# Splitting matmuls into column halves: gate and value products of one token block, down products of the next

## Chip, cores and metric

The kernel runs on one core of a Trainium2 chip. The metric is the device time of one execution in microseconds (us), as a median of several runs. A separate profiled execution gives the rows that are shown below.

## What is computed

Attention over four sequences of 768 tokens with eight heads of 64, and a gated MLP on its output. Each query sees the keys less than 16 positions away, and one pooled key (maximum) and value (mean) per block of 32 positions. The MLP takes the 3072 tokens of 512 features to 1536 and back. Cut to what matters:

```python
x = attention(q, k, v)                      # 3072 tokens x 512
g = x @ w_gate                              # 3072 x 1536
silu = g * (1.0 / (1.0 + np.exp(-g)))
val = x @ w_val
out = (silu * val) @ w_out                  # 3072 x 512
```

## The kernel before

The 3072 tokens go in six blocks k = 0 to 5 of TOK = 512. Within a block, attention leaves x transposed: features on the 128 partitions, in NP = 4 tiles u, the 512 tokens along the free dimension. Each tile is held as a rounded part `xh` and the rest `xl`, both fp32r (a 4-byte type that TensorE takes in a single pass). The weights are held in the same two parts, `wh` and `wl`, and a product is made of three terms: `wl·xh`, `wh·xl`, `wh·xh`.

The 1536 hidden features go in NJ = 12 tiles j of 128. For each (k, j):

- `m_gate` calls `m_up` (L609) for the gate product: 4 tiles u with 3 terms each, 12 matmuls (L619) that add up in one PSUM tile `g` of 128 x 512. The weights are the stationary operand (128 x 128), x the moving one (512 token columns). ScalarE then applies Silu to the whole tile (L625) and leaves `a` in SBUF.
- `m_val` does the same with the value weights into a tile `v`, multiplies `a` by it on VectorE (L630), rounds `a` to `ah` on ScalarE (through the helper at L187) and leaves the rest `al` on GpSimd (helper at L183).
- `m_down` (L660) multiplies `ah` and `al` with the 128 rows of w_out that belong to j: for each of NTP = 4 groups i of 128 tokens three terms, 12 matmuls (L669). Here the activations are stationary and w_out is the moving operand with DM = 512 output columns. The sums stay in four PSUM tiles `acc` over all twelve j; after j = 11 they are copied out and stored.

From block 1 on a loop writes the order by hand: gate (k, j), some attention steps of a later block, value (k, j), more attention steps, the down products of the (k, j) before, and again attention steps. A manual dependency on every instruction keeps this order on each engine. Block 0 follows a list of steps of its own. The attention steps for block k + 1 lie between the products of block k; block 5 has none.

PSUM has two buffers for g and v (`psg`), two for attention (`psy`) and four for the sums (`psc`). The weights stay in SBUF for the whole run; those of j = 11 lie in a pool of their own (`wts3`), opened late, and the gate and value weights of j = 0 and 11 are separate tiles (`w_g`, `w_v`) where the other j share one (`w_gv`).

Every matmul in the program comes with a weight load (LDWEIGHTS, engine PEld in the profile). At the start, and while the first attention steps wait, the kernel runs fillers: matmuls of a tile of plain fp32 zeros with 128 to 512 columns (`zeros`, L693).

Of the kernel before, what the change touches and what calls it, by code (L numbers as in the profile page):

```python
# [18 lines left out]
DM = H * D  # L19
DFF = 1536  # L20
BLK, WIN = 32, 16
P = 128
NP = H // 2
# [9 lines left out]
TOK = 512  # L33
# [3 lines left out]
NJ = DFF // P  # L37
# [3 lines left out]
WARM = (4, 3)  # L41
OWN = (0,)
SHORT = 2
QC = P // NP
ODD = NT // 2
EVEN = 1 + ODD
# [33 lines left out]
def blocks_of(k):  # L80

    return [(b, pos, i * QT // SQ + x, n * QT // SQ) for x, (b, pos, i, n) in enumerate(parts_of(k))]


def parts_of(k):


    found, at = [], k * TOK
    while at < (k + 1) * TOK:
        b, pos = divmod(at, S)  # L90
        n = min(S - pos, (k + 1) * TOK - at)
        found.append((b, pos, (at - k * TOK) // QT, n // QT))
        at += n
    return found


def value_pool() -> np.ndarray:

    m = np.zeros((P, NV, QC), np.float32)
    for i in range(WIN, WIN + S):  # L100
# [62 lines left out]
def body(ctx, tc, qP, kP, vT, vP, kq, kF, qF, vE, vR, vO, wgv, wends, wo, cst_in, bias_in, out):  # L163
    nc = tc.nc
# [20 lines left out]
    def copy(e, out, in_):  # L185
        if e == "a":
            nc.scalar.copy(out, in_)  # L187
        else:
            (nc.vector if e == "d" else nc.gpsimd).tensor_copy(out, in_)
# [64 lines left out]
    KT, VT, ksum, vsum, X, U = {}, {}, {}, {}, {}, {}  # L254
# [39 lines left out]
    def a_load_windows(k, u):  # L294
        if k >= SHORT:
            parts = blocks_of(k)
            kw = two.tile([P, TOK // SQ + len(parts), SB], F32, tag="kw", name=f"kw_{k}_{u}")
            for b, pos, i, n in parts:
                nc.sync.dma_start(
                    kw[:, i : i + n + 1, :SQ],  # L300
                    kP[b, u][:, pos : pos + (n + 1) * SQ].rearrange("p (n j) -> p n j", j=SQ),
                )
            U.setdefault((k, u), {})["kw"] = kw
            return
        kw = two.tile([P, NT, KC], F32, tag="kw", name=f"kw_{k}_{u}")
        for b, pos, i, n in parts_of(k):
            src = kP[b, u]
            nc.sync.dma_start(
                kw[:, i : i + n, :KW], bass.AP(src.tensor, src.offset + pos, [[PADS, P], [QT, n], [1, KW]])
            )  # L310
        U.setdefault((k, u), {})["kw"] = kw
# [29 lines left out]
    def a_keys(k, u):  # L341
        for b, pos, i, n in parts_of(k) if k < SHORT else blocks_of(k):
            if pos == 0:
                a_pool_keys(u, 0)
            kw = U[k, u]["kw"]
            copy(
                "p",
                kw[:, i : i + n, KW:] if k < SHORT else kw[:, i : i + n, SQ:],
                ksum[u].rearrange("p (o n) -> p o n", o=1).broadcast_to([P, n, NB]),
            )  # L350
# [23 lines left out]
    def v_rows():  # L374
        if "rows" not in vn:
            t = pro.tile([P, (EVEN + NV - 1) * DM + NV * QC], F32, name="vrows")
            vn["flat"] = t
            vn["rows"] = t[:, : (EVEN + NV - 1) * DM].rearrange("p (n d) -> p n d", d=DM)
        return vn["rows"]

    def v_even(i):
        return 0 if i == NV - 1 else EVEN + i

    def v_sums():
# [3 lines left out]
        for i in range(NV):  # L388
            n = P if i < NV - 1 else VREST
            for u in range(NP):  # L390
                nc.tensor.matmul(  # L391
                    ps[u * QC : (u + 1) * QC, :P], mean_sb[:n, i, :], v_rows()[:n, v_even(i), u * P : (u + 1) * P],
                    start=i == 0, stop=i == NV - 1,
                )

    def v_keep():

        ps = vn.pop("sums")
        for u in range(NP):
            copy(on, vsum["all"][KW:, u * P : (u + 1) * P], ps[u * QC : u * QC + NB, :P])  # L400

# [9 lines left out]
    def a_scores(k, u):  # L411
        t = U[k, u]
        sc = [a_bank(k, u, f"sc{h}", "yg"[h]) for h in range(2)]
        t["sc"] = sc
        if k >= SHORT:
            for b, pos, at, n in blocks_of(k):
# [48 lines left out]
    def a_max(k, u, g):  # L465

        t = U[k, u]
        if g == 0 and k >= SHORT:
            t["p"] = short["p"]
# [6 lines left out]
        for c in range(NTP):  # L476
            i = g * NTP + c
            n = (k * NTP + c) % (S // P)
            kc = KC if k < SHORT else SC
            v = 0 if n == 0 else 2 if n == S // P - 1 else 1  # L480
# [126 lines left out]
    A, ACC = {}, {}  # L607

    def m_up(k, j, nm, pairs=range(NP)):  # L609

        if pairs[0] == 0:
            A[nm, k, j] = psg.tile([P, 512], F32, tag="b", name=f"{nm}_{k}_{j}")
        ps = A[nm, k, j]
        wh, wl = W[nm, j]
        for u in pairs:
            xh, xl = X[k, u]
            cs = slice(u * P, (u + 1) * P)
            for n, (w, x) in enumerate(((wl, xh), (wh, xl), (wh, xh))):
                nc.tensor.matmul(  # L619
                    ps, w[:, cs], x, start=u == 0 and n == 0, stop=u == NP - 1 and n == 2  # L620
                )
# [22 lines left out]
    def m_up_gate(k, j, *u):  # L644
        m_up(k, j, "g", *([u] if u else []))

    def m_up_val(k, j, *u):
        m_up(k, j, "v", *([u] if u else []))
# [11 lines left out]
    def m_down(k, j):  # L660
        if j == 0:
            ACC[k] = [psc.tile([P, DM], F32, tag="b", name=f"acc{i}_{k}") for i in range(NTP)]
        ah, al = A.pop((k, j))
        wh, wl = W["o", j]
        for i in range(NTP):
            ts = slice(i * P, (i + 1) * P)
            terms = ((al, wh), (ah, wl), (ah, wh)) if k < NBLK - 1 else ((ah, wh), (ah, wl), (al, wh))
            for n, (a, w) in enumerate(terms):
                nc.tensor.matmul(  # L669
                    ACC[k][i], a[:, ts], w, start=j == 0 and n == 0, stop=j == NJ - 1 and n == 2  # L670
                )
            if j == NJ - 1:
                r = k * TOK + i * P
                parts = 2 if k == NBLK - 1 and i == NTP - 1 else 1
                for h in range(parts):
                    n = DM // parts
                    cs = slice(h * n, (h + 1) * n)
                    if parts == 1:
                        o = mlp.tile([P, n], F32, tag="o", bufs=3, name=f"o_{k}_{i}")
                    else:  # L680
                        o = mlp.tile([P, TOK], F32, tag="a", name=f"o_{k}_{i}_{h}")[:, :n]
                    copy("ad"[(i + h) % 2], o, ACC[k][i][:, cs])
                    nc.sync.dma_start(out[r : r + P, cs], o)
# [76 lines left out]
    for n in WARM:  # L760
# [10 lines left out]
        "out": a_out, "outp": a_out_pooled, "split": a_split, "rest": a_rest, "w_load": w_load, "w_abs": w_abs, "w_c1": w_range,  # L771
        "w_c2": w_shift, "w_s1": w_top, "w_s2": w_rest, "w_hi": w_hi, "w_lo": w_lo, "gate": m_up_gate,
        "silu": m_silu, "val": m_up_val, "mul": m_mul, "ah": m_high, "al": m_low, "down": m_down,
        "values": a_values, "load_values": a_load_values, "keys": a_keys, "pool_values": a_pool_values,
        "exp": a_exp, "norm": a_norm,
# [48 lines left out]
    for n, (k, j) in enumerate(seq):  # L824
        m_gate(k, j)
        do(3 * n)
        m_val(k, j)
        do(3 * n + 1)
        if prev:
            m_down(*prev)  # L830
        do(3 * n + 2)
        prev = (k, j)
    m_down(*prev)
    assert not at
    for x in traced[n_before:]:
# [48 lines left out]
```

## Time and profile before

| | |
|---|---|
| median of 3 runs | 678.6 us (678.54 to 678.86) |
| time of the profiled execution | 678.02 us |
| span of the profiled execution, first to last instruction | 676.2 us |
| mean granted TensorE clock | 0.999 of full speed |
| PE (TensorE matmul) busy | 670.1 us |
| PEld (weight load) busy | 543.5 us |
| DVE (VectorE) busy | 331.3 us |
| ACT (ScalarE) busy | 298.1 us |
| POOL (GpSimd) busy | 134.4 us |

The span leaves out what lies around the program, 1.8 us here. Matmuls overlap in the record, because the recorded duration of one holds its latency; how densely they stand is read from their starts.

### The profile page before, as it was taken

The page shows a single profiled execution, that of the slowest core. Times are in us where ns is not written, and L with a number is a line of the kernel's source. Part 1 is how long each engine was busy: PE and PEld are TensorE (multiplying, and loading weights), DVE is VectorE, ACT ScalarE, POOL GpSimd, SP SyncE. Part 2 cuts the span into 40 slices and gives each one's busy share as a digit, 9 for nine tenths or more (in the row PEclk, how much of TensorE's full clock was granted, in tenths as well). Part 3 has the DMA queues.
Part 4 walks back from the last instruction along what each step waited for, and adds up shares of the span by engine and source line. Part 5 has one row for each costly group of instructions (what it writes and reads, how often), then busy time and mean ns, then how long its engine had stood idle before and what let it go on. Part 6 is the DMA issues. An engine that isn't in the chain of part 4 may idle for free.

```text
span 676.2 us, 12388 instructions
## 1 busy us (share of the span) xinstructions
PE 670.1 (99%) x4940; PEld 543.5 (80%) x4940; DVE 331.3 (49%) x919; ACT 298.1 (44%) x729; POOL 134.4 (20%) x130
## 2 busy tenths in 40 slices
PE   8999999999999999999999999999999999999997
PEld 5688888888888888888888888888888888888886
DVE  6999999946624525435346345343352451100011
ACT  6968998844441433424415424235244151211112
POOL 3110112112221212212112122121212121111110
PEclk9999999999999999999999999999999999999999
DMA  8899165145320223302404312012122000100001
GB/s 328 340 373 354 49 234 171 46 120 157 79 58 0 56 48 95 82 24 55 105 24 143 80 49 58 18 38 64 56 57 57 0 25 0 63 1 0 1 0 63
DMA packets 72058, 60.36 MB, mean 89 GB/s; under 512 B 42144, under 2 KB 60064, under 8 KB 70464
## 3 DMA queue, kind: packets, MB, share of 16 engines
q1 hardware_dynamic: 72000, 59.57, 28.6%
q8 instruction: 39, 0.64, 0.4%
q14 instruction: 19, 0.16, 0.1%
HBM read 53.26 MB, written 6.29 MB: 88 GB/s over the span
## 4 chain that ended last, share of the span: by engine, by line
PE 97%; DVE 2%; DMA 1%; issue 0%; SPq 0%; ACT 0%; DVEq 0%; ACTq 0%
PE g L619 30%; PE acc L669 29%; PE v L619 29%; PE xo L584 4%; PE sc L423 2%; DMA kq<-in_kF 1%; PE pp L537 1%; DVE p L481 1%; PE sc L434 1%; PE xo L592 1%; DVE ks L336 0%; PE pv L391 0%; PE pp L693 0%; PE pv L370 0%; DVE m_g L221 0%
## 5 line engine op out<-in xcount | busy, mean ns | idle before, releaser
L669 PE MATMUL acc<-w_o,ah 128*128 128x512 f32 x576 | 177.7, 390 | 0.0
L619 PE MATMUL g<-xh,w_gv 128*128 128x512 f32 x480 | 160.3, 395 | 0.0
L619 PE MATMUL v<-xh,w_gv 128*128 128x512 f32 x480 | 158.0, 390 | 0.0
L183 POOL TENSOR_TENSOR al<-a,ah 128x512 fp32r<-128x512 f32 x63 | 81.7, 1296 | 333.4 <-ACT ah L187 333.4
L630 DVE TENSOR_TENSOR a<-v,a 128x512 f32<-128x512 f32 x72 | 49.7, 690 | 191.6 <-PE v L619 190.8
L669 PEld LDWEIGHTS acc<-w_o,ah 128*128 128x128 f32 x576 | 108.1, 188 | 22.7
L187 ACT CAST ah<-a 128x512 fp32r<-128x512 f32 x71 | 44.0, 621 | 156.8 <-DVE a L630 156.8
L669 PE MATMUL acc<-w_o,al 128*128 128x512 f32 x288 | 113.0, 392 | 0.0
L619 PEld LDWEIGHTS g<-xh,w_gv 128*128 128x128 f32 x480 | 90.1, 188 | 21.1 <-ACT w_o L187 0.2
L619 PEld LDWEIGHTS v<-xh,w_gv 128*128 128x128 f32 x480 | 90.1, 188 | 19.1 <-issue 0.3
L625 ACT ACTIVATE a<-g 128x512 f32<-128x512 f32 x72 | 43.0, 597 | 137.9 <-PE g L619 136.3
L565 DVE STREAM_TRANSPOSE pt_short<-p_short 32x256 f32<-32x256 f32 x192 | 83.8, 436 | 25.9 <-POOL p_short L522 23.2
L619 PE MATMUL g<-xl,w_gv 128*128 128x512 f32 x240 | 93.5, 390 | 0.0
L619 PE MATMUL v<-xl,w_gv 128*128 128x512 f32 x240 | 93.4, 389 | 0.0
L669 PEld LDWEIGHTS acc<-w_o,al 128*128 128x128 f32 x288 | 54.1, 188 | 11.5 <-issue 0.2
L619 PEld LDWEIGHTS v<-xl,w_gv 128*128 128x128 f32 x240 | 45.1, 188 | 9.3
L619 PEld LDWEIGHTS g<-xl,w_gv 128*128 128x128 f32 x240 | 45.1, 188 | 8.8
L496 ACT ACTIVATE p_short<-p_short,nm 128x88 f32<-128x88 f32 x128 | 45.3, 355 | 0.2
L522 POOL TENSOR_TENSOR p_short<-p_short,ri 128x704 f32<-128x704 f32 x16 | 21.8, 1364 | 57.5 <-DVE ri L514 53.6
L619 PE MATMUL g<-xh,w_g 128*128 128x512 f32 x96 | 32.6, 400 | 0.0
L619 PE MATMUL v<-xh,w_v 128*128 128x512 f32 x96 | 31.9, 393 | 0.0
L187 ACT CAST xh<-xo 128x512 fp32r<-128x512 f32 x23 | 13.4, 591 | 38.2 <-PE xo L584 38.2
(108 smaller groups left out, 690.9 us busy)
## 6 DMA issues: line engine op xcount, KB each, us to landing
raw_gv<-in_wgv SPq DMA_DIRECT2D x10, 1024.0 KB, 11.8
raw_o<-in_wo SPq DMA_DIRECT2D x12, 512.0 KB, 7.4
out<-o SPq DMA_DIRECT2D x23, 256.0 KB, 2.0
kt<-in_kP SPq DMA_DIRECT2D x12, 384.0 KB, 4.1
vt<-in_vT SPq DMA_DIRECT2D x12, 384.0 KB, 3.9
vw<-in_vP SPq DMA_DIRECT2D x12, 384.0 KB, 3.8
kw<-in_kP SPq DMA_DIRECT2D x12, 272.0 KB, 4.7
vw<-in_vP SPq DMA_DIRECT2D x16, 192.0 KB, 3.4
```

Source lines behind the costliest of these rows:

```text
L183: (nc.vector if e == "d" else nc.gpsimd).tensor_tensor(out=out, in0=a, in1=b.bitcast(F32), op=ALU.subtract)
L187: nc.scalar.copy(out, in_)
L423: nc.tensor.matmul(sc[h][s * SQ : (s + 1) * SQ, c * SC : (c + 1) * SC], t["q"][hs, i * SQ : (i + 1) * SQ], keys[hs], start=True, stop=True,)
L434: nc.tensor.matmul(sc[h][s * QT : (s + 1) * QT, c * KC : (c + 1) * KC], t["q"][hs, qs], t["kw"][hs, i, :], start=True, stop=True,)
L496: nc.scalar.activation(out=t["p"][:, i, :kc], in_=t["p"][:, i, :kc], func=AF.Exp, scale=-1.0, bias=t["nm"][:, i : i + 1], accum_out=t["sm" ...
L522: (nc.vector if on == "d" else nc.gpsimd).tensor_tensor(out=p, in0=p, in1=ri.rearrange("p (n o) -> p n o", o=1).broadcast_to([P, 2 * NTP, ...
L565: nc.vector.transpose(out=to[r * SQ : (r + 1) * SQ, :, s * SQ : (s + 1) * SQ], in_=t["p"][s * SQ : (s + 1) * SQ, :, at : at + SQ],)
L584: nc.tensor.matmul(ps[hs, qs], vw, t["pt"][:n, h, qs], start=k not in OWN or i == 0, stop=k not in OWN)
L619: nc.tensor.matmul(ps, w[:, cs], x, start=u == 0 and n == 0, stop=u == NP - 1 and n == 2)
L625: nc.scalar.activation(out=a, in_=A.pop(("g", k, j)), func=AF.Silu)
L630: nc.vector.tensor_tensor(out=a, in0=ps, in1=a, op=ALU.mult)
L669: nc.tensor.matmul(ACC[k][i], a[:, ts], w, start=j == 0 and n == 0, stop=j == NJ - 1 and n == 2)
```

## The change

In block 3 each gate and value product is made in two halves of 256 token columns: first all twelve matmuls for the left half of the PSUM tile, then all twelve for the right half. In block 4 each down product of a token group is made in two halves of 256 output columns: the three terms of the left half, then those of the right half. The tiles, the terms and their order within a half, and the work on other engines stay as they are. The start flag of a down sum is given for the left half of j = 0 alone.

```diff
+HALVES = (3, 4)
...
         ps = A[nm, k, j]
         wh, wl = W[nm, j]
+        if k == HALVES[0]:
+            for h in range(2):
+                hs = slice(h * TOK // 2, (h + 1) * TOK // 2)
+                for u in pairs:
+                    xh, xl = X[k, u]
+                    cs = slice(u * P, (u + 1) * P)
+                    for n, (w, x) in enumerate(((wl, xh), (wh, xl), (wh, xh))):
+                        nc.tensor.matmul(
+                            ps[:, hs], w[:, cs], x[:, hs], start=u == 0 and n == 0, stop=u == NP - 1 and n == 2
+                        )
+            return
...
-            for n, (a, w) in enumerate(terms):
-                nc.tensor.matmul(
-                    ACC[k][i], a[:, ts], w, start=j == 0 and n == 0, stop=j == NJ - 1 and n == 2
-                )
+            for h in range(2 if k == HALVES[1] else 1):
+                hs = slice(h * DM // 2, (h + 1) * DM // 2) if k == HALVES[1] else slice(0, DM)
+                for n, (a, w) in enumerate(terms):
+                    nc.tensor.matmul(
+                        ACC[k][i][:, hs], a[:, ts], w[:, hs],
+                        start=j == 0 and n == 0 and h == 0, stop=j == NJ - 1 and n == 2 and h == len(range(2 if k == HALVES[1] else 1)) - 1,
+                    )
```

## Rows read from the trace of the kernel before

**Rows 1.** The page: span, busy time of PE, granted clock in 40 slices.
```profile
span 676.2 us, 12388 instructions
...
PE 670.1 (99%) x4940; PEld 543.5 (80%) x4940; DVE 331.3 (49%) x919; ACT 298.1 (44%) x729; POOL 134.4 (20%) x130
...
PEclk9999999999999999999999999999999999999999
```

**Rows 2.** The page, chain that ended last: shares by engine and by line.
```profile
PE 97%; DVE 2%; DMA 1%; issue 0%; SPq 0%; ACT 0%; DVEq 0%; ACTq 0%
PE g L619 30%; PE acc L669 29%; PE v L619 29%; PE xo L584 4%; PE sc L423 2%; DMA kq<-in_kF 1%; PE pp L537 1%; DVE p L481 1%; PE sc L434 1%; PE xo L592 1%; DVE ks L336 0%; PE pv L391 0%; PE pp L693 0%; PE pv L370 0%; DVE m_g L221 0%
```

**Rows 3.** Busy time by stretch, blocks 3 and 4 (stretch, its length, busy by engine).
```profile
core 0: us, PE busy (x) PEld busy (x) DVE busy (x) ACT busy (x) POOL busy (x), PEclk, DMA share, GB/s
357.60:465.10 107.50, 107.50 (x829) 87.94 (x820) 49.21 (x153) 41.07 (x107) 23.50 (x23) 1.00 0.23 61
465.10:571.20 106.10, 106.10 (x761) 87.10 (x752) 42.28 (x141) 39.29 (x101) 22.46 (x19) 1.00 0.16 41
```

**Rows 4.** The same, matmuls and loads of line 619 alone (PE, PEld).
```profile
357.60:465.10 107.50, 68.37 (x288) 53.45 (x288) 1.00 0.23 61
```

**Rows 5.** The same, matmuls and loads of line 669 alone (PE, PEld).
```profile
465.10:571.20 106.10, 34.68 (x144) 27.03 (x144) 1.00 0.16 41
```

**Rows 6.** Chain in order of time, block 3: start us, us, what.
```profile
383.76 0.89 PE sc L423 x60
...
393.03 2.72 PE g L619 x12
395.75 2.72 PE v L619 x12
```

**Rows 7.** Chain in order of time, block 5 (down of j = 8; gate, value of j = 11).
```profile
650.53 2.72 PE acc L669 x12
...
661.42 2.79 PE g L619 x12
664.21 2.80 PE v L619 x12
```

**Rows 8.** Timeline from 620 us: start us, us, engine, line, operation, out<-in.
```profile
620.45 0.39 PE L619 MATMUL g<-xh,w_gv 128*128 128x512 f32 x1
620.45 0.19 PEld L619 LDWEIGHTS g<-xl,w_gv 128*128 128x128 f32 x1
620.67 0.39 PE L619 MATMUL g<-xl,w_gv 128*128 128x512 f32 x1
```

**Rows 9.** Timeline of the weight loads, fillers (512 columns, then 128).
```profile
13.59 0.19 PEld L693 LDWEIGHTS pp<-warm 128*128 128x128 f32 x1 [0.24 <-issue]
14.02 0.19 PEld L693 LDWEIGHTS pp<-warm 128*128 128x128 f32 x1 [0.24 <-issue]
14.13 0.90 PEld L537 LDWEIGHTS pp<-consts,p 128*120 128x120 f32 x8
```

**Rows 10.** Timeline of PE, two fillers of 256 columns in a row.
```profile
10.42 0.38 PE L693 MATMUL sc<-warm 128*128 128x256 f32 x1
...
10.64 0.38 PE L693 MATMUL sc<-warm 128*128 128x256 f32 x1
```

**Rows 11.** Timeline of the weight loads around one of 24 columns.
```profile
266.22 0.19 PEld L669 LDWEIGHTS acc<-w_o,ah 128*128 128x128 f32 x1
266.45 0.09 PEld L370 LDWEIGHTS pv<-consts,vr 128*24 128x24 f32 x1
266.68 0.19 PEld L619 LDWEIGHTS g<-xh,w_gv 128*128 128x128 f32 x1
```

**Rows 12.** All waits of PEld, 357.6 to 571.2 us (PE has none).
```profile
PEld xo L584 <- issue: 2.8, 8, 0.4
```

**Rows 13.** The page, groups: what follows a value tile (mean ns after busy).
```profile
L183 POOL TENSOR_TENSOR al<-a,ah 128x512 fp32r<-128x512 f32 x63 | 81.7, 1296 | 333.4 <-ACT ah L187 333.4
L630 DVE TENSOR_TENSOR a<-v,a 128x512 f32<-128x512 f32 x72 | 49.7, 690 | 191.6 <-PE v L619 190.8
...
L187 ACT CAST ah<-a 128x512 fp32r<-128x512 f32 x71 | 44.0, 621 | 156.8 <-DVE a L630 156.8
```

## The prediction

> **What bounds the kernel now.** I read the page first. [...] PE makes up 97% of the chain that ended last, and three groups make up 88% of that chain: gate products, value products and down products [rows 2]. The reader is to see there that the order of products on PE is the whole path.
>
> Then I cut the span into stages. From 357.6 to 465.1 us (block 3) and from 465.1 to 571.2 us (block 4) PE is busy for every one of the 107.5 and 106.1 us, while DVE is busy for 49.2 and 42.3, ACT for 41.1 and 39.3 and POOL for 23.5 and 22.5 [rows 3]. In both stages no PE matmul waits for another engine; the only wait on the weight side is 2.8 us of issue ahead of the attention's own products [rows 12]. So nothing in these stages can absorb time that PE gains, and every nanosecond added to a product there is added to the end.
>
> A busy PE says little about how densely its products stand, so the next view is the chain in order of time. Twelve products of 512 columns take 2.72 us, gate and value alike [rows 6], down products too [rows 7]: 2.72 / 12 = 226.7 ns from one to the next. [...] The recorded 390 ns of one product is latency and is not used.
>
> **The change, part by part.**
>
> *The count.* Block 3 has 288 gate and value products [rows 4]; a block has 144 down products, which is what the second stretch shows [rows 5]. All 432 become two of 256 columns. Columns streamed stay the same. What is added is 432 matmuls and, because the code has a weight load for each matmul and orders the terms so that neighbours differ in weights, 432 weight loads.
>
> [...]
>
> *What a matmul costs beyond its columns.* This is the unknown; no product in this trace of the single-pass kind (fp32r) has other than 512 columns. [...] Two rows speak on which kind it is. First, weights at another place (j = 11) lengthen products whose moving data is the same as for every other j [rows 7]: an excess that hangs on the load, of which there is one per matmul, whatever its columns. Second, against a price by weight columns: the load of only 24 columns at 266.45 us is followed by the next load at 266.68, again 0.23 us [rows 11]. Together: an excess that comes once per matmul and does not shrink with its size. I take 13.3 ns as fixed, with no certainty, and keep zero as the lower end.
>
> [...]
>
> *Weight loads.* Today a load starts at the moment at which the matmul before it starts (both at 620.45) and has 0.22 us until its own at 620.67 [rows 8]. After the change it has 0.12. The record says 0.19 us for a load [rows 8], which would not fit; but that holds latency. Among the fillers a load of 128 columns starts at 14.02 us beside a matmul of 107 ns, and the next load, which starts with the matmul that uses the first, stands at 14.13 [rows 9]: 0.11 us is enough. So the load just fits into 120 ns and I cost it at nothing. Its cover is the 106.7 ns of the other half; if the cover does not hold, the upper end is 0.19 us a half, 432 x (380 - 227) = 66 us.
>
> *Issue.* 60 score products pass in 0.89 us [rows 6], 15 ns each, so PE's queue delivers far faster than one product in 120 ns. Nothing.
>
> *Other engines.* The activation of a gate tile and the product with a value tile wait for the whole tile, as before, so they start when the second half's last product ends. After a value tile come 0.69, 0.62 and 1.30 us on DVE, ACT and POOL [rows 13], 2.6 together, and the down products that need them stand behind the next j's gate and value products, 2 x 2.72 us. That cover grows with the change. Sums in PSUM go to the same banks, read at the same points; no transfer is moved and no new wait arises. Nothing.
>
> *The sum.* 396 products x 13.3 ns = 5.3 us, and the 36 of j = 11 x 19.5 ns = 0.7 us: 6.0 us. On the profiled execution's 678.0 us that gives 684.0. The runs shown have a median 0.6 above that execution, so the median is forecast at 684.6; for a single number I give 684.5.
>
> **The rivals.**
>
> *The excess goes with the columns* (not slower). Then a matmul costs what plain ones do, 2 ns, and the remaining 224.4 ns of a product halve: 112.2 + 2.3 = 114.5, a pair 229.0, and 432 x 2.3 = 1.0 us: 679.6; with no fixed part at all, 678.6. For it speaks that plain matmuls show a fixed cost of only 2 to 3 ns [rows 9, 10], against it the longer products of j = 11, whose columns are the same. It decides if halves stand less than about 115 ns apart. [...]
>
> *The load does not fit* (much slower). [...] It is hidden up to 120 ns; from there each 10 ns more cost 432 x 20 ns = 8.6 us. At the recorded 0.19 us the time is 745. Against it: no product shows an exposed load in a steady row [rows 6]. [...]
>
> *The split gains.* Nothing in the rows gives a half a lower price than half a product. I keep 4 in 100 for what I have not seen.
>
> **How the numbers follow.** Fixed excess: 0.60, at 683 to 687. With the columns: 0.24, at 678.6 to 679.8. Load exposed: 0.12, from 686 upwards. Gain: 0.04. About 0.2%, 1.4 us, is what a measurement of this kernel can tell from no change, so "same" ends at 680.0. Same is then 0.22 (most of the second case), slower 0.74 (the first, the third and a remainder of the second), faster 0.04. The range runs from 679.0, which takes in the part of the second case with a small fixed cost, to 690, which takes in a load that outlasts its cover by some 5 ns; outside lie the gain, the second case's lowest end and the long loads, about 2 in 10.
>
> **What would show it.** In the chain by time, gate and value pieces of block 3 and down pieces of block 4 with 24 matmuls in 2.88 us (2.75 if the excess goes with the columns, 3.0 or more if loads are exposed); in the timeline, halves 0.120 us apart, each load starting with the matmul before it; block 3 longer by 4.0 us and block 4 by 2.0; PE still without waits; all else unchanged. Wrong would be: halves at 0.113 to 0.115 us, halves that stand 0.19 apart, a split whose two halves differ, or a change of time outside these two blocks.

## The result

The changed kernel takes 683.59 us (median of 3 runs, 682.97 to 683.76) against 678.6 us before: a ratio of 1.007, 95% interval 1.0047 to 1.0093. It is slower by 5.0 us; the forecast was 684.5, in a range of 679 to 690. The profiled execution took 682.97 us, with a span of 681.2 us.

**The page.** PE has 432 matmuls and 432 loads more than in [rows 1], and is as full as before.

```profile
span 681.2 us, 13253 instructions
PE 674.8 (99%) x5372; PEld 566.0 (83%) x5372; DVE 331.0 (49%) x919; ACT 298.3 (44%) x729; POOL 134.2 (20%) x130
...
PEclk9999999999999999999999999999999999999999
```

**Where the time went.** The chain in order of time gives the starts of three gate products, each the first of its block: block 3 and block 4, then block 5. First the kernel before:

```profile
357.71 2.94 PE g L619 x12
...
465.21 2.95 PE g L619 x12
...
571.30 2.94 PE g L619 x12
```

and after the change:

```profile
357.19 3.07 PE g L623 x24
...
468.30 2.99 PE g L631 x12
...
576.25 2.95 PE g L631 x12
```

Block 3 went from 107.50 to 111.11 us (+3.61) and block 4 from 106.09 to 107.95 (+1.86), 5.47 in all. The rest is a start that is 0.52 us earlier after the change (357.19 against 357.71). It arises in block 0, before any changed instruction, and differs from one trace to the next. 5.47 - 0.52 is the difference of the two spans, 5.0. Of block 4's down products the twelve of j = 11 lie behind the start of block 5; they added nothing, as the rows on j = 11 below show.

**The pieces.** The answer to [rows 6] in block 3 (start us, us, what), and to the down products in block 4:

```profile
388.10 2.88 PE v L623 x24
390.98 2.75 PE acc L683 x12
393.73 2.87 PE g L623 x24
396.60 2.88 PE v L623 x24
...
482.29 2.87 PE acc L683 x24
```

24 matmuls of 256 columns take 2.88 us, 120.0 ns each, where 12 of 512 took 2.72, 226.7 each. So 256 columns more take 106.7 ns, 0.417 a column, and 13.3 ns are left at either width. The whole down products that follow halves take 2.75 us: in the timeline their first five stand 228 to 236 ns apart, and only the later ones return to 227. Such a change of width costs about 0.03 us.

**The loads.** The timeline answers [rows 8]:

```profile
396.44 0.28 PE L623 MATMUL v<-xh,w_gv 128*128 128x256 f32 x1
396.56 0.28 PE L623 MATMUL v<-xl,w_gv 128*128 128x256 f32 x1
...
396.44 0.19 PEld L623 LDWEIGHTS v<-xl,w_gv 128*128 128x128 f32 x1
396.56 0.31 PEld L623 LDWEIGHTS v<-xh,w_gv 128*128 128x128 f32 x2
```

A load still starts with the matmul before its own (396.44), and its own starts 0.12 us later (396.56), although the record gives the load 0.19. From 357 to 470 us PE waits for no engine, and PEld as before [rows 12] for issue alone, ahead of the attention's products:

```profile
PEld xo L585 <- issue: 1.4, 4, 0.4
```

**j = 11.** Its gate and value pieces, 2.79 and 2.80 us as whole products in block 5 [rows 7], are 2.84 as halves:

```profile
457.90 2.84 PE g L623 x24
460.74 2.84 PE v L623 x24
```

The down products of j = 11 of block 4, before and after the change:

```profile
576.97 2.80 PE acc L669 x12
```

```profile
581.92 2.80 PE acc L683 x24
```

Twelve whole products and their 24 halves take the same 2.80 us: here the split was free.

### The profile page after: what moved, and what is told of

It reads as the page before. It is cut to its first block, busy times and chain, and to the rows that moved or that the text cites. A ratio compares the mean times of both kernels' runs of the same rounds, so it can differ in the third digit from the quotient of the medians.

```text
span 681.2 us, 13253 instructions
## 1 busy us (share of the span) xinstructions
PE 674.8 (99%) x5372; PEld 566.0 (83%) x5372; DVE 331.0 (49%) x919; ACT 298.3 (44%) x729; POOL 134.2 (20%) x130
## 4 chain that ended last, share of the span: by engine, by line
PE 97%; DMA 1%; DVE 1%; SPq 0%; issue 0%; ACT 0%; DVEq 0%; ACTq 0%
PE acc L683 29%; PE g L631 25%; PE v L631 24%; PE g L623 5%; PE v L623 5%; PE xo L585 4%; PE sc L424 2%; DMA raw_g<-in_wends 1%; PE pp L538 1%; PE sc L435 1%; PE xo L593 1%; PE pv L392 0%; PE pp L708 0%; PE pv L371 0%; DVE p L482 0%
## 5 line engine op out<-in xcount | busy, mean ns | idle before, releaser
L683 PE MATMUL acc<-w_o,ah 128*128 128x512 f32 (+1 forms) x672 | 183.3, 360 | 0.0
L631 PE MATMUL g<-xh,w_gv 128*128 128x512 f32 x400 | 133.6, 395 | 0.0
L631 PE MATMUL v<-xh,w_gv 128*128 128x512 f32 x400 | 131.7, 390 | 0.0
L683 PE MATMUL acc<-w_o,al 128*128 128x512 f32 (+1 forms) x336 | 121.6, 362 | 0.0
L631 PEld LDWEIGHTS g<-xh,w_gv 128*128 128x128 f32 x400 | 75.2, 188 | 17.4 <-ACT w_o L188 0.2
L631 PEld LDWEIGHTS v<-xh,w_gv 128*128 128x128 f32 x400 | 75.1, 188 | 15.7
L631 PE MATMUL g<-xl,w_gv 128*128 128x512 f32 x200 | 78.2, 391 | 0.0
L631 PE MATMUL v<-xl,w_gv 128*128 128x512 f32 x200 | 77.9, 389 | 0.0
L623 PE MATMUL g<-xh,w_gv 128*128 128x256 f32 x160 | 30.9, 287 | 0.0
L623 PE MATMUL v<-xh,w_gv 128*128 128x256 f32 x160 | 30.4, 283 | 0.0
```

The lines of the kernel that those rows point to most:

```text
L623: nc.tensor.matmul(ps[:, hs], w[:, cs], x[:, hs], start=u == 0 and n == 0, stop=u == NP - 1 and n == 2)
L631: nc.tensor.matmul(ps, w[:, cs], x, start=u == 0 and n == 0, stop=u == NP - 1 and n == 2)
L683: nc.tensor.matmul(ACC[k][i][:, hs], a[:, ts], w[:, hs], start=j == 0 and n == 0 and h == 0, stop=j == NJ - 1 and n == 2 and h == len(rang ...
```

## The experiments

The first six kernels, and the changed one without the 32 bytes near the end, are the changed kernel with the widths made a table; `UP` gives the widths of gate and value products by block, `DOWN` those of the down products. The change itself is `UP = {3: (256, 256)}` and `DOWN = {4: (256, 256)}`.

```diff
+        if k in UP:
+            edges = np.cumsum((0, *UP[k]))
+            for lo, hi in zip(edges, edges[1:]):
+                hs = slice(int(lo), int(hi))
...
+            edges = np.cumsum((0, *DOWN.get(k, (DM,))))
+            for lo, hi in zip(edges, edges[1:]):
+                hs = slice(int(lo), int(hi))
```

The kernel before ran beside each set on the same chip: 677.94 us with one part alone and the two uneven splits; 677.99 with the quarters, all blocks and the two kernels without the 32 bytes; 678.52 with the halves side by side, the 2-byte type and the moved x tiles.

### One part alone

```diff
-DOWN = {4: (256, 256)}
+DOWN = {}
```

> Block 3's half of the change alone (288 gate and value products as two of 256 columns). If each matmul costs 13.3 ns beyond its columns whatever its size, gate and value pieces of block 3 stay at 24 matmuls in 2.88 us and the time rises by 288 x 13.3 ns = 3.8 us at most, less what j = 11 does not show in the changed kernel: about 3.5 us above before. If the two parts hide or cause each other's cost, the rise is not the share 3.5 of 5.5.

Measured: 682.04 us, ratio 1.0057 (1.0045 to 1.007), 4.1 us above the median of before. A gate piece of block 3 reads

```profile
394.69 2.87 PE g L625 x24
```

```diff
-UP = {3: (256, 256)}
+UP = {}
```

> Block 4's half alone (144 down products as two of 256 columns). Fixed cost: 24 matmuls in 2.87 us, 144 x 13.3 ns = 1.9 us above before, and with the other half alone the two sum to the whole change. If the cost came from the moving operand being the tokens (block 3) and not from the matmul count, this one would be within 0.5 us of before.

Measured: 680.46 us, ratio 1.0034 (1.0021 to 1.0046), 2.5 us above. The down piece:

```profile
561.34 2.87 PE acc L686 x24
```

Each part costs its own share, whether the tokens or the weights stream. The two excesses sum to 6.6 us, above the 5.0 of the change itself; their intervals are about 0.8 us wide on either side, and the pieces are the same in all three traces, so the traces are the better measure of the shares: block 3 takes 111.1 us in the first kernel and block 4 107.95 in the second, as in the changed kernel, so 3.6 and 1.9.

### 320 + 192 columns

```diff
+UP = {3: (320, 192)}
+DOWN = {4: (320, 192)}
```

> The same 432 products split 320 + 192, same number of matmuls. Pure fixed cost: 146.7 and 93.3 ns, a pair 240.0, the time of the changed kernel (683.6). Fixed cost with the load as a floor at the fillers' 0.109 us (my expectation): the run of twelve 192-column matmuls takes 1.31 us in place of 1.12, a pair 255.7, 432 x 29 ns = 12.5 us above before, about 691. If the 120 ns of the even halves is itself a load that does not fit: twelve of 192 columns in 1.44 us, a pair 266.7, about 696.

Measured: 693.1 us, ratio 1.0223 (1.0207 to 1.0239), 15.2 us above the before of its set, between the second case (12.5) and the third (432 x 40 = 17.3). The spacings decide. The timeline of PE in a value product, three matmuls of 320 and nine of 192 between the rows' starts:

```profile
399.84 0.46 PE L625 MATMUL v<-xh,w_gv 128*128 128x320 f32 x2
...
400.28 0.46 PE L625 MATMUL v<-xh,w_gv 128*128 128x320 f32 x2
...
401.07 0.39 PE L625 MATMUL v<-xh,w_gv 128*128 128x192 f32 x2
...
402.07 0.27 PE L625 MATMUL v<-xh,w_gv 128*128 128x192 f32 x1
```

0.44 / 3 = 147 ns for 320 columns: 133.3 at 0.417 ns a column, and 13.3. 1.00 / 9 = 111 ns for 192 columns, where 93.3 would follow from columns and the fixed part. So at 192 columns something else sets the pace at 111 to 112 ns. It is close to the 0.11 us of a load beside a filler [rows 9]; but that filler's own 128 columns last about as long (from 128 to 512 columns the spacing in [rows 9] grows by 0.32 us, 107 ns for each 128), so its row shows only that a load needs no more. That the load sets the pace fits and is not shown: no fp32r matmul without a load was run. The even halves, at 120, stand above that floor and are not set by it.

### 272 + 240 columns

```diff
+UP = {3: (272, 240)}
+DOWN = {4: (272, 240)}
```

> The same 432 products split 272 + 240. The spacings seen so far, 226.7 and 120.0 ns, are 17 and 9 steps of 13.3 ns. Fixed cost of 13.3 ns per matmul: 126.7 and 113.3 ns, a pair 240.0, as the changed kernel (683.6). Spacing rounded up to whole steps of 13.3 ns after some 2.5 ns of its own: 115.8 to 120.0 and 102.5 to 106.7, a pair 226.7, so no cost, 678.6 (240 columns then perhaps held at 109 by the load, 679.6). The load as the limit of the even halves at 120: 126.7 + 120, a pair 246.7, 687.

Measured: 686.28 us, ratio 1.0121 (1.0107 to 1.0135), 8.3 us above the before of its set. By the time alone that is the third case (432 x 20 = 8.6 us). The trace says otherwise; first the chain in order of time:

```profile
404.37 2.86 PE g L625 x24
407.23 2.85 PE v L625 x24
```

12 pairs in 2.85 us are 238 ns a pair: not 226.7 (2.72 us) and not 246.7 (2.96). The timeline has the two widths apart, the first and the last of a value piece's twelve 272s (the last in one row with the first 240), then the second and the last of its twelve 240s:

```profile
407.07 0.29 PE L625 MATMUL v<-xh,w_gv 128*128 128x272 f32 x1
...
408.45 0.40 PE L625 MATMUL v<-xh,w_gv 128*128 128x272 f32 x2
408.69 0.27 PE L625 MATMUL v<-xl,w_gv 128*128 128x240 f32 x1
...
409.81 0.27 PE L625 MATMUL v<-xh,w_gv 128*128 128x240 f32 x1
```

1.38 / 11 = 125 ns for 272 columns, 12 beyond the 113.3 of the columns; 1.12 / 10 = 112 ns for 240, 12 beyond 100. Steps of 13.3 ns and a load limit of 120 both fall. The fixed part is met within 1 to 2 ns: 272 columns should take 126.7 by it and 240 should take 113.3, and in this piece both came out a little under, which no floor explains. 240 columns run at the pace of 192. The rest of the time is a new wait, so that the time came near the third case by chance. From 357 to 470 us PE has one that neither of the two kernels has:

```profile
PE v L625 <- DVE a L644: 2.6, 4, 0.7
```

Four times a value product stands until VectorE has multiplied the value tile of the j before, which holds the PSUM buffer. The timeline of DVE in this kernel, and in the changed one at the same j:

```profile
392.25 5.38 DVE L567 STREAM_TRANSPOSE pt_short<-p_short 32x256 f32<-32x256 f32 x12 [1.55 <-POOL p_short L524]
397.67 0.69 DVE L644 TENSOR_TENSOR a<-v,a 128x512 f32<-128x512 f32 x1
```

```profile
391.00 1.33 DVE L566 STREAM_TRANSPOSE pt_short<-p_short 32x256 f32<-32x256 f32 x3 [1.54 <-POOL p_short L523]
392.37 0.69 DVE L642 TENSOR_TENSOR a<-v,a 128x512 f32<-128x512 f32 x1
```

With other widths the program was built with the multiplication behind all twelve transposes in place of three. So 2.6 of the 8.3 us come from this order and not from what the matmuls of the two widths cost.

### Quarters

```diff
+UP = {3: (128,) * 4}
+DOWN = {4: (128,) * 4}
```

> The same 432 products in four matmuls of 128 columns. Pure fixed cost: 4 x 66.7 = 266.7 ns a product, 48 matmuls in 3.20 us, 432 x 40 ns = 17 us above before, 696. With the load as a floor at 0.109 us (my expectation): 4 x 109 = 436 ns, 48 in 5.23 us, 432 x 209 = 90 us, about 769. Floor at 120: 48 in 5.76 us, 109 us, about 787.

Measured: 773.29 us, one run, 95 us above before.

```profile
390.39 5.36 PE v L625 x48
```

5.36 / 48 = 112 ns each, with 53.3 ns of columns and 66.7 by the fixed part: the pace of the 192s again, and 432 x (447 - 227) = 95 us is the whole difference. If it is the load's, this is the price that the prediction kept as the second rival; it was met at 240, 192 and 128 columns, and not at 256.

### All blocks

```diff
+UP = {k: (256, 256) for k in range(1, 6)}
+DOWN = {k: (256, 256) for k in range(1, 6)}
```

> Halves of 256 columns for all 2160 gate, value and down products of blocks 1 to 5. Fixed cost: 1980 x 13.3 ns = 26.3 us, and the 180 products of j = 11 at the some 2 ns that the changed kernel shows: 26.7 us, 705, with block 5 at 2.88 us a piece like block 3. If the cost needs something of blocks 3 and 4 (the attention between the products), block 5, which has none, stays at 2.72 and the sum is some 5 us less.

Measured: 704.38 us, ratio 1.0389 (1.0373 to 1.0405), 26.4 us above before, against 26.7 expected. Block 5, which has no attention beside its products:

```profile
649.56 2.88 PE acc L686 x24
652.44 2.88 PE g L625 x24
655.32 2.88 PE v L625 x24
```

Five times as many products give five times the cost, and the attention work has no part in it.

### Halves of a term side by side

Every second matmul now has the weights of the one before it, in the down products as well (not shown below); each still has its load, 5372 of either as in the changed kernel. In the sums of both halves the start flag stands on the first matmul alone.

```diff
-                for u in pairs:
-                    xh, xl = X[k, u]
-                    cs = slice(u * P, (u + 1) * P)
-                    for n, (w, x) in enumerate(((wl, xh), (wh, xl), (wh, xh))):
+            for u in pairs:
+                xh, xl = X[k, u]
+                cs = slice(u * P, (u + 1) * P)
+                for n, (w, x) in enumerate(((wl, xh), (wh, xl), (wh, xh))):
+                    for h in range(2):
+                        hs = slice(h * 256, (h + 1) * 256)
...
```

> The change with the two halves of a term next to each other, so that every second matmul has the weights of the one before it; the number of matmuls and of loads stays. If the 13.3 ns belong to each matmul with its load, nothing changes: 24 matmuls in 2.88 us and 683.6. If they belong to a switch to other weights, a pair costs 106.7 + 106.7 + 13.3 = 226.7, 24 in 2.72 us, and the time is that of before.

Measured: 683.47 us, ratio 1.0077 (1.0062 to 1.0092).

```profile
388.51 2.88 PE v L624 x24
```

Nothing changes. The cost is not one of switching to other weights; whether a load of the same weights costs it is not separated here.

### A 2-byte type in place of fp32r

Gate and value products of blocks 3 and 4 are left out; matmuls of the constant identity's bits, read as bf16, stand in their place. The down products are whole.

```diff
+            one_bit = id_sb.bitcast(BF16)
+            twice = one_bit.rearrange("p (o n) -> p o n", o=1).broadcast_to([P, 2, 256])
+            for hs in (slice(0, 512),) if k == 3 else (slice(0, 256), slice(256, 512)):
...
+                            ps[:, hs].rearrange("p (o n) -> p o n", n=256), one_bit[:, n % 2 * P : (n % 2 + 1) * P],
+                            twice if k == 3 else twice[:, :1], start=u == 0 and n == 0, stop=u == NP - 1 and n == 2
```

> Block 3 and block 4 leave out their gate and value products: in their place stand as many matmuls of a 2-byte type (bf16, the bits of the constant identity tile, both operands), 512 columns in block 3 and 256 in block 4, each with a load; the down products stay. If 13.3 ns come with every matmul and load of whatever type: 226.7 and 120.0 ns, 12 in 2.72 us and 24 in 2.88 us. If they come from streaming four bytes a column: about 216 and 109 ns, 12 in 2.59 us and 24 in 2.62 us.

Measured: 672.34 us, one run. Value pieces of block 3 (12 of 512 columns) and block 4 (24 of 256):

```profile
360.67 2.59 PE v L624 x12
```

```profile
464.70 2.62 PE v L624 x24
```

215.8 and 109.2 ns: 256 columns more take 106.6 ns, as for fp32r, and about 2.5 ns are left at either width. All 864 of these matmuls had a load (count, and shortest, median and longest duration in ns):

```profile
L624 PEld LDWEIGHTS <-consts x864: 95/98/100, 357.9 to 561.4; 128*128 128x128 bf16 x173
```

So a stream at the same pace of columns, with a load before each matmul, need not cost 13.3 ns. But these loads last 98 ns in the record where those of fp32r last 188, and the data are mostly zeros. Two rows of the kernel before speak on the load. The plain fp32 fillers, with loads of 0.19 us, stand 0.43, 0.22 and 0.11 us apart at 512, 256 and 128 columns [rows 9, 10], or 429, 216 and 109 ns by the starts in the trace: 213 ns for 256 columns, half the speed of fp32r, and only 2 to 3 beyond them. And the fp32r product beside the load of 24 columns, 0.09 us long, still takes 0.23 [rows 11]: a shorter load beside it does not take the 13.3 away. Together they put the 13.3 on fp32r, either its stream or the taking in of its own weights. Which of the two is not shown.

### Why j = 11 is slow

A program listing of SBUF places puts the weights of j = 11 at byte 216736 and up of each partition, 32 bytes past a multiple of 64; all others start on a multiple of 64. Two kernels remove the 32 bytes, one made from the kernel before and one from the changed kernel:

```diff
-            vr = two.tile([P, NB], F32, tag="vr", name=f"vr_{k}_{u}")
+            vr = two.tile([P, 32], F32, tag="vr", name=f"vr_{k}_{u}")[:, :NB]
```

> The kernel before with one buffer made 32 bytes longer, which moves the weights of j = 11 from an address 32 bytes past a multiple of 64 to a multiple of 64. If the address makes their products slower, gate, value and down pieces of j = 11 fall from 2.79 to 2.72 us; 216 products x 6.2 ns = 1.3 us less than before, 677.3. If j = 11 is slow for its place in the order (the sums are copied out around it), nothing changes: 678.6.

Measured: 678.12 us, ratio 1.0003 (0.9994 to 1.0012). Gate and value of j = 11 in block 3:

```profile
454.81 2.81 PE g L619 x12
457.62 2.80 PE v L619 x12
```

The down products of j = 11 of block 4, which were 2.80 before (the row at 576.97 above):

```profile
576.87 2.76 PE acc L669 x12
```

> The changed kernel with the same 32 bytes. If the address is the reason why the halves of j = 11 take 117.6 ns in place of 120 and its whole products 233 in place of 227: block 3's gate and value pieces of j = 11 rise from 2.83 to 2.88 us, the whole products of j = 11 elsewhere fall to 2.72, together 1.0 us less than the changed kernel, 682.6. Otherwise both stay.

Measured: 683.5 us, ratio 1.0083 (1.0069 to 1.0096).

```profile
459.60 2.83 PE g L625 x24
462.43 2.83 PE v L625 x24
```

The gate and value pieces moved in neither, so the 32 bytes are not the reason for theirs. The down piece did fall, 2.80 to 2.76, half of the way to 2.72: there the weights are the moving operand, and its offset counts. It does not always: in the changed kernel without the 32 bytes the whole down piece of j = 11 that stands between halves, at 364.85, still took 2.80. The last kernel moves the x tiles up, which brings the weights of j = 11 down:

```diff
-    att = pool("att", 2)
+    att = pool("att", 2, side="right")
```

> The kernel before with the x tiles moved from byte 76928 to byte 196576 and up of each partition; the weights of j = 11 move down from 216736 to 183968. If products are slower whose operands lie in the upper part (as those of j = 11 do, at 216736 and up), all gate and value products go to 233 ns (12 in 2.79 us) and the down products of j = 11 to 227: some 1440 x 6.2 ns less 72 x 5 ns, 8.5 us above before. If j = 11 is slow for another reason, nothing changes: 678.

Measured: 689.6 us, ratio 1.0166 (1.0149 to 1.0183), 11.1 us above before where 8.5 was expected. A value piece in block 2:

```profile
338.95 2.80 PE v L619 x12
```

2.80 in place of 2.72: with x moved, the gate and value products take 6 to 7 ns more. The rest of the 11.1 us is in the down pieces behind them, 2.77 in place of 2.72 in the first row below (a change of pace costs, as after halves). But j = 11 does not fit. Here is the end of block 5: the down products of j = 9, gate and value of j = 11, and the last two down pieces, j = 10 and 11:

```profile
670.25 2.77 PE acc L669 x12
673.01 2.75 PE g L619 x12
675.76 2.75 PE v L619 x12
678.52 5.58 PE acc L669 x24
```

Gate and value of j = 11 read the same x at the same high place and take 2.75, not 2.80. The last two down pieces were 5.54 in the kernel before and did not get shorter, although the weights of j = 11 came down. And the new place of x, byte 196576, is itself 32 bytes past a multiple of 64, so this kernel changed place and offset together. What the runs show is that the places of both operands matter, by up to 7 ns a product; a rule for which places are slow does not come out of them, and why j = 11 is slow stays open.

## Why the prediction was right, and where it was off

**What bounds the kernel** held. PE stayed without waits, and all that was added to its products came out at the end.

**The unknown term** held. No run of before shows the 13.3 ns that the sum uses: its fp32r products with 226.7 ns all have 512 columns, which does not tell what part goes with the columns; the 13.3 were the author's estimate. In its place the changed kernel showed 120.0 ns at 256 columns: 106.7 for 256 columns, and 13.3 beside them. A fixed part of 13.3 ns was met again at 320 columns (147 ns), and within 1 to 2 ns at 272 (125 ns). The rival by columns wanted 2.75 us a piece and is out. The reason given was weaker than the conclusion: that weights of j = 11 lengthen products was read as an excess that hangs on the load. The run with x moved shows the same lengthening when the moving operand changes place, and the split itself shows that the excess of j = 11 does shrink with size (see the sum). The second reason, the load of 24 columns [rows 11], stands. So one of the two reasons for a fixed price was false, and to that extent the conclusion was lucky; the chance of 0.60 left room for it. What carries the conclusion are the widths.

**Weight loads** held: at 256 columns they fit, as the row at 14.13 us said. That 240, 192 and 128 columns all ran at 111 to 112 ns fits a load that needs about as long. The recorded 0.19 us is no limit: the loads at 396.44 and 396.56 stand 0.12 us apart, each starting together with a matmul.

**Issue and other engines** held in this change. That they could have failed is shown by 272 + 240: the cover of the multiplication on VectorE depends on where the program's build puts it among the transposes, and there it cost four stalls, 2.6 us.

**The sum** was 0.5 us too large: 6.0 against 5.47 (3.61 where 4.0 was foreseen for block 3, 1.86 where 2.0 was for block 4). The step that was mis-sized is the term of the 36 products of j = 11, taken as 19.5 ns each, 0.70 us; no run shows the 19.5, and in its place the term measured 0.1 us. The gate and value pieces grew by 0.05 us each, from 2.79 and 2.80 to 2.84, 0.1 us of the 0.47 set down for block 3, and the down piece, 2.80 before and after, by nothing of its 0.23. The excess of j = 11 over the other j is not per matmul: whole it is 6 ns, halved it is gone in this kernel (2.84 us a piece against 2.88). Two smaller terms were not in the sum: the first gate product after attention grew by 0.13 us and not 0.16 (2.94 to 3.07), and each return from halves to whole products costs 0.03 us.

**The median** came out 0.9 us below the forecast of 684.5: 0.5 from this sum. The remaining 0.4 is no more than the start of a run varies by, and the medians of before in the later sets lie 0.1 to 0.7 below its 678.6.

## What to carry to other kernels

Find the price of a matmul beyond its columns before splitting it, from starts and not from recorded durations, and for the type in use: here it is 13.3 ns for fp32r and 2.5 ns for bf16, so every fp32r matmul of 512 columns that was cut into halves, but for those of j = 11, cost 13.3 ns more where PE is the bound. At 240, 192 and 128 columns each fp32r matmul with its load took 111 to 112 ns whatever its size, so quarters cost far more, 95 us. After a change of widths look at the order of the other engines too: it may be built anew and bring a wait that has nothing to do with the change, 2.6 us with 272 + 240.

## What was not expected of the hardware

What twelve fp32r products take depends on where both operands lie in SBUF: 2.72, 2.75 or 2.80 us. An offset of 32 bytes from a multiple of 64 counts for the moving operand in the down products of j = 11 (2.80 with it, 2.76 without, in the kernel before). After a change from halves to whole products the first five stand 228 to 236 ns apart before they settle at 226.7. What in fp32r costs the 13.3 ns is open; an fp32r matmul without a load was not tried.
